# Windowed attention and a gated feed-forward: two weight loads moved in the queue, one normalising pass for two head pairs, diagonals on two engines, and a new table of order

## Chip, core and metric

One core of a Trainium2 chip. Five engines run side by side: TensorE (PE) multiplies matrices into PSUM, VectorE (DVE), ScalarE (ACT) and GpSimd (POOL) work elementwise, SyncE (SP) issues transfers. The metric is the device time of one execution in microseconds (us).

## What is computed

The kernel takes q, k and v (8 batches, 8 heads, 576 positions, 64 wide) and three weights, and gives 8 x 576 x 512 numbers.

```python
# attention: window of 32 positions to each side
scores = q @ k.T / 8
scores = where(abs(i - j) <= 32, scores, -1e9)
attn   = exp(scores - max) ; attn /= sum(attn) + 1e-9
x      = (attn @ v), heads side by side            # (8, 576, 512)
# feed-forward with a convolution of three positions in the gate
h    = relu(x @ w_in)                              # w_in: 512 x 1024
c    = conv_w[0]*h[s-1] + conv_w[1]*h[s] + conv_w[2]*h[s+1]
out  = (h * sigmoid(c)) @ w_out                    # w_out: 1024 x 512
```

## The kernel before

**Attention** (`attention`, L755) runs for one batch at a time, in two halves `s` of 288 positions. SP loads q and k (`load_qk`, L494, two loads for each half) and v (`load_v`, L524) in float32 into staging tiles `qst`, `kst` and `vst`. `cast_qk`, `cast_v` and `shift_v` turn them into bf16 tiles `qn`, `kn`, `ve` and `vo`, where `vo` is v moved by 64 rows; for batch 0 any of three engines may do it, later POOL alone. `transposes` (L583) turns q and k on PE (L597) and copies them from PSUM into `qT` and `kT`. `scores` (L624) multiplies a tile of 64 queries by 128 keys on PE (L657). The mask is put on in one of three ways: PE adds a band before the exp (L646), or POOL or DVE multiplies by a 0/1 mask after it (L679). ACT takes the exp (L672) into `attn`. `values` (L682) multiplies by v with a column of ones beside it (L700), so that the sum of a row stands in column 64 of 65. DVE takes the reciprocal (L719) and multiplies each of the two head pairs of a PSUM slot by it, one pass for each (L722), into `xn`. `turn` (L729) transposes `xn` into `xT`: on PE (L744) for batches 0 and 1, by a transfer (L735) for the others.

**Feed-forward** (`hidden`, L797) runs over 12 chunks of 384 positions, three chunks for two batches. Chunks 0 and 1 are cut into two pieces. For each of eight blocks `m` of 128 channels, PE multiplies `xT` by `w_in` (L835), ACT takes the relu into `hT` (L851), and the three taps of the convolution are dealt out in one of six ways (`KINDS`, L792): PE with a diagonal matrix (L872), ACT with a scale (L902), DVE by multiply and add in PSUM (L909), or POOL in `tmp` (L888, L893). ACT takes the tanh (L914; the sigmoid as a tanh of half the argument) and DVE forms the gate (L917) into `gT`. `project` (L929) multiplies by `w_out` on PE (L940), copies the result to `y` (L395 or L401), and SP writes it out (L960, L956).

The diagonals (24 matrices of 128 x 128, `diag_w`) are built at the start by `conv_weights` (L468, L483) on DVE. `load_w` (L558) loads w_in and w_out in two halves each into the staging tiles `wst` and casts them (L578). `copy` (L393) does all copies and casts, so in the profile L395 is ACT, L397 POOL and L401 DVE.

**What sets the order.** All of this only records operations with what they read and write. Four tables at the top then fix everything: `ORDER` (the order in which operations are issued, L29), `PICK` (the engine of those that have a choice), `BANKS` (the PSUM bank of each slot) and `CHOICE` (the way of the mask or of the taps). `Plan.place` (L263) walks through `ORDER`, gives each operation an engine and a bank and computes a start time by costs written beside each operation; the instructions are then issued in order of these start times, so the costs decide how the queues interleave. Each engine works through its queue in that order and waits on semaphores for what it needs. `warm` (L966) puts spare matmuls (L969) where PE would stand idle in the first 36 us of the plan. SP's loads go through one queue, with eight semaphores in turn: a transfer waits for the one eight places before it. A load into a staging tile also waits until the tile's last contents have been cast.

In the first part of SP's queue stand q and k of both halves of batch 0, v of both halves (six loads), then the two halves of w_in as the 15th and 16th load. The loads of batch 1 and of w_out follow.

Of the kernel before, what the change touches and what calls it, by code (L numbers as in the profile page):

```python
# [9 lines left out]
FP32 = mybir.dt.float32  # L10
BF16 = mybir.dt.bfloat16
AF = mybir.ActivationFunctionType
ALU = mybir.AluOpType
# [4 lines left out]
    0, 0, 0, 0, 0, 2, 0, 2, 0, 2, 5, 5, 0, 0, 5, 5, 5, 5, 5, 5, 5, 5, 5, 0, 5, 5, 2, 2, 2, 0, 0, 5,  # L18
    5, 5, 1, 5, 5, 5, 5, 2, 5, 5, 5, 1, 0, 5, 2, 0, 0, 0, 0, 0, 2, 2, 3, 2, 0, 2, 1, 3, 0, 1, 2, 2,
    1, 5, 0, 3, 0, 0, 0, 2, 2, 2, 2, 3, 2, 2, 0, 2, 3, 0, 2, 2, 0, 1, 2, 2, 1, 4, 2, 0, 2, 3, 0, 5,  # L20
    3, 2, 2, 0, 2, 0, 0, 2, 0, 2, 2, 3, 2, 3, 2, 2, 1, 2, 3, 2, 2, 0, 2, 1, 2, 2, 2, 0, 2, 3, 3, 1,
    2, 3, 3, 2, 2, 2, 3, 2, 2, 3, 2, 0, 2, 2, 3, 2, 3, 2, 2, 3, 0, 2, 2, 3,
]
SUPERSET = False
WARM = (5.0, 36.0)
# [4 lines left out]
    27, 34, 28, 35, 45, 46, 0, 1, 2, 3, 10, 30, 29, 36, 37, 51, 17, 26, 25, 14, 24, 22, 49, 52, 50,  # L30
    47, 48, 5, 12, 23, 11, 70, 69, 72, 77, 76, 87, 88, 7, 55, 56, 32, 42, 79, 71, 78, 89, 90, 93,
    91, 92, 53, 54, 94, 99, 100, 95, 96, 4, 97, 98, 39, 31, 38, 13, 33, 44, 16, 41, 21, 43, 61, 73,
    80, 62, 64, 57, 58, 59, 9, 60, 63, 65, 67, 74, 81, 75, 82, 84, 15, 83, 40, 85, 86, 105, 115,
    117, 116, 119, 101, 102, 66, 68, 118, 224, 225, 220, 221, 106, 108, 20, 107, 226, 227, 242, 222,
    223, 103, 120, 122, 124, 230, 231, 121, 228, 229, 234, 235, 246, 104, 111, 123, 232, 233, 250,
    236, 18, 243, 247, 244, 112, 6, 19, 248, 8, 113, 114, 237, 238, 138, 135, 142, 145, 137, 144,
    153, 136, 143, 155, 156, 151, 239, 249, 259, 253, 152, 251, 256, 154, 245, 240, 252, 241, 109,
    157, 158, 260, 261, 176, 177, 140, 182, 183, 194, 195, 257, 258, 110, 266, 267, 190, 191, 392,
    393, 162, 163, 396, 397, 386, 387, 262, 263, 159, 160, 388, 389, 390, 264, 265, 394, 398, 274,
    400, 270, 402, 391, 275, 401, 254, 271, 395, 405, 399, 408, 411, 161, 412, 268, 416, 139, 149,  # L40
    146, 147, 419, 406, 255, 409, 422, 403, 413, 404, 420, 410, 281, 278, 417, 418, 421, 414, 423,
    425, 179, 178, 310, 311, 284, 415, 424, 317, 141, 282, 283, 407, 269, 150, 164, 165, 287, 290,
    285, 286, 167, 166, 426, 427, 168, 169, 170, 171, 328, 279, 280, 291, 324, 325, 313, 312, 318,
    326, 327, 174, 175, 172, 272, 273, 288, 276, 277, 184, 185, 192, 196, 173, 428, 429, 297, 289,
    329, 430, 330, 300, 444, 431, 148, 293, 298, 292, 301, 130, 134, 132, 449, 331, 197, 445, 299,
    302, 294, 450, 446, 447, 451, 448, 193, 295, 296, 180, 188, 131, 186, 133, 125, 128, 126, 127,
    129, 303, 304, 351, 314, 319, 350, 355, 362, 363, 366, 432, 433, 335, 332, 333, 349, 348, 354,
    364, 367, 360, 361, 365, 334, 475, 336, 337, 203, 204, 368, 201, 202, 369, 307, 308, 476, 181,
    187, 189, 315, 320, 322, 316, 323, 338, 339, 342, 198, 199, 205, 340, 341, 436, 437, 200, 440,
    441, 434, 435, 452, 343, 453, 454, 442, 458, 443, 321, 455, 345, 344, 438, 439, 483, 482, 485,  # L50
    489, 496, 463, 497, 459, 500, 467, 460, 461, 484, 490, 498, 502, 503, 352, 358, 464, 462, 468,
    501, 469, 456, 457, 465, 466, 521, 520, 525, 305, 306, 536, 537, 532, 353, 357, 359, 518, 519,
    524, 534, 530, 531, 499, 506, 507, 533, 535, 206, 207, 209, 208, 371, 372, 210, 211, 373, 374,
    504, 505, 538, 539, 370, 212, 356, 375, 213, 376, 378, 379, 542, 543, 377, 487, 492, 380, 382,
    486, 494, 491, 381, 540, 541, 488, 495, 508, 509, 510, 512, 218, 219, 214, 215, 216, 217, 470,
    511, 513, 515, 514, 523, 527, 493, 522, 528, 529, 526, 544, 545, 546, 547, 548, 549, 559, 560,
    555, 556, 571, 557, 471, 550, 551, 472, 558, 473, 563, 561, 562, 564, 588, 572, 576, 474, 569,
    570, 573, 574, 682, 683, 689, 719, 718, 724, 734, 735, 477, 478, 684, 685, 690, 702, 703, 700,
    567, 589, 577, 590, 591, 723, 721, 720, 581, 582, 725, 583, 584, 585, 575, 568, 593, 736, 737,
    565, 566, 608, 701, 602, 592, 607, 609, 610, 687, 692, 383, 594, 586, 603, 595, 597, 479, 604,  # L60
    605, 732, 733, 347, 384, 346, 623, 596, 598, 587, 621, 696, 624, 641, 480, 622, 599, 578, 697,
    642, 698, 699, 629, 630, 600, 625, 626, 730, 731, 637, 606, 601, 633, 656, 627, 611, 638, 643,
    612, 613, 862, 823, 686, 694, 631, 688, 824, 830, 841, 693, 579, 580, 634, 664, 837, 628, 644,
    632, 842, 657, 691, 635, 636, 665, 614, 616, 658, 666, 645, 646, 667, 695, 825, 826, 831, 838,
    651, 647, 648, 652, 653, 309, 615, 649, 650, 669, 668, 659, 639, 640, 660, 654, 655, 743, 744,
    617, 618, 619, 839, 840, 745, 740, 706, 727, 670, 671, 741, 742, 661, 843, 844, 707, 738, 739,
    704, 705, 722, 726, 728, 729, 750, 751, 385, 753, 752, 517, 1025, 516, 757, 1027, 827, 863, 672,
    746, 747, 748, 749, 662, 758, 867, 845, 846, 878, 879, 663, 708, 709, 710, 847, 848, 712, 713,
    714, 763, 761, 764, 711, 673, 762, 790, 759, 760, 849, 715, 765, 766, 828, 835, 1026, 553, 832,
    1032, 1043, 833, 1044, 829, 834, 861, 836, 850, 1028, 860, 795, 674, 851, 853, 854, 855, 852,  # L70
    778, 675, 773, 755, 481, 676, 1033, 857, 856, 779, 796, 774, 767, 768, 866, 876, 877, 1045,
    1046, 677, 771, 769, 780, 781, 775, 776, 678, 784, 783, 785, 786, 787, 772, 800, 788, 770, 797,
    798, 791, 864, 870, 756, 1170, 1029, 554, 810, 809, 811, 1041, 804, 777, 782, 801, 1042, 792,
    799, 802, 793, 679, 680, 812, 813, 805, 789, 806, 807, 803, 874, 875, 552, 899, 900, 1064, 1065,
    1069, 808, 903, 904, 814, 907, 905, 1039, 901, 915, 906, 925, 908, 794, 865, 871, 930, 931, 932,
    815, 916, 1080, 1081, 902, 1076, 1077, 920, 816, 868, 620, 1030, 926, 917, 918, 1040, 927, 928,
    933, 934, 919, 929, 921, 935, 936, 922, 817, 818, 819, 1049, 1050, 1047, 1048, 1051, 872, 913,
    914, 717, 1031, 1035, 1037, 1038, 923, 909, 910, 873, 1034, 1056, 1052, 911, 912, 869, 1036,
    820, 937, 946, 821, 1053, 716, 754, 1057, 1059, 1055, 1054, 1058, 924, 947, 951, 952, 1062, 859,
    1210, 885, 886, 883, 884, 1063, 1068, 953, 954, 887, 955, 942, 938, 939, 940, 943, 944, 965,  # L80
    966, 1078, 1079, 941, 967, 968, 969, 970, 1074, 1075, 880, 881, 945, 948, 892, 893, 894, 895,
    971, 972, 1066, 1172, 1171, 1173, 1178, 988, 981, 949, 982, 882, 950, 983, 989, 985, 984, 1087,
    1088, 956, 975, 976, 973, 1186, 1177, 1188, 990, 991, 974, 1174, 1067, 1071, 992, 1072, 888,
    1190, 1000, 957, 986, 1187, 1191, 1189, 958, 977, 1175, 681, 959, 1070, 1073, 889, 891, 890,
    1089, 993, 1001, 987, 1002, 1084, 1085, 1082, 1083, 1180, 994, 1086, 1003, 1004, 960, 1094,
    1095, 1096, 1090, 1005, 961, 979, 995, 822, 1211, 978, 1208, 1209, 1176, 898, 858, 1212, 1179,
    1214, 1182, 1215, 980, 1183, 1181, 1184, 1185, 1009, 1097, 996, 997, 998, 1091, 1093, 1092,
    1099, 896, 1098, 1100, 897, 962, 963, 1060, 1006, 999, 1010, 1101, 1102, 1118, 1107, 1117, 1119,
    1120, 1224, 1195, 1007, 1108, 1225, 1121, 1011, 1196, 1105, 1106, 1130, 1014, 1008, 1015, 1197,
    1016, 1017, 1103, 1104, 1226, 1222, 1223, 1012, 1220, 1221, 1113, 1111, 1112, 1114, 1136, 1109,  # L90
    1110, 1129, 1131, 1132, 1133, 1013, 1227, 1122, 1202, 1203, 1205, 1115, 1116, 1151, 1020, 1018,
    1157, 1218, 1156, 1158, 1159, 1213, 1217, 1137, 1138, 1139, 1204, 1123, 1152, 1124, 1125, 1021,
    1141, 1022, 1019, 1153, 1154, 1126, 1127, 1134, 1142, 1146, 1023, 1024, 1061, 1219, 1155, 1128,
    1143, 1147, 1192, 1193, 1144, 1135, 1247, 1248, 1160, 1249, 1250, 1230, 1253, 1255, 1231, 1148,
# [951 lines left out]
```

## Time and profile before

| what | us |
|---|---|
| median of 13 runs | 224.06 |
| lowest and highest run | 222.55, 226.05 |
| the profiled run | 224.06 |
| its span in the profile | 222.2 |
| PE busy (share of the span) | 201.3 (91%) |
| DVE busy | 192.8 (87%) |
| ACT busy | 185.9 (84%) |
| POOL busy | 182.7 (82%) |
| loads and stores moved | 45.92 MB, 207 GB/s on the mean |

The profile is that of one execution. Busy time of PE counts a matmul from its start to its modelled end, so neighbours overlap and a busy PE need not be at its peak. In a row of instructions the busy time is the union of the row's instructions, and the mean in ns is that of one instruction alone; where instructions follow each other directly, busy time divided by their number is a little less than the mean. The clock of PE was granted at full speed except in the stretch from 10 to 20 us (0.83).

### The profile page before, as it was taken

The numbers are of one execution on the slowest core, as the hardware profiler recorded it, in microseconds if no ns is written. First come the engines' busy times: TensorE is split into PE (matmuls) and PEld (weight loads), VectorE is DVE, ScalarE is ACT, GpSimd is POOL, SyncE is SP. The second block draws the span as 40 slices with busy tenths as digits, with TensorE's granted clock in tenths as the row PEclk, the third lists the DMA queues.
The fourth block names the chain that finished last, engine by engine and source line by source line (L and its number), as shares of the span: only waits on it lengthen the run. The fifth ranks groups of instructions, "written<-read, shape, count | busy, mean of one in ns | idle before, by whom it ended". The sixth has DMA issues, their size and how long they took to land.

```text
span 222.2 us, 6471 instructions
## 1 busy us (share of the span) xinstructions
PE 201.3 (91%) x2451; PEld 127.0 (57%) x2469; DVE 192.8 (87%) x430; ACT 185.9 (84%) x388; POOL 182.7 (82%) x234
## 2 busy tenths in 40 slices
PE   1768899888999799999999999789999999999994
PEld 0535688775677566646655556446646555455542
DVE  6769794797698799999999989799999999999970
ACT  2239679777989599999899989988999989999962
POOL 4267577979889989799999998999998999999930
PEclk9997999999999999999999999999999999999999
DMA  5999999998998899999999989963537313130334
GB/s 175 302 181 388 361 274 331 307 236 247 290 185 244 261 150 230 338 216 204 246 228 249 230 205 273 342 194 78 83 83 256 101 62 118 25 143 3 142 117 167
DMA packets 68675, 45.92 MB, mean 207 GB/s; under 512 B 53644, under 2 KB 53924, under 8 KB 68644
## 3 DMA queue, kind: packets, MB, share of 16 engines
q1 hardware_dynamic: 68608, 45.49, 78.9%
q8 instruction: 19, 0.31, 0.6%
q14 instruction: 12, 0.10, 0.1%
q10 hardware_dynamic: 36, 0.01, 0.0%
HBM read 32.52 MB, written 9.44 MB: 189 GB/s over the span
## 4 chain that ended last, share of the span: by engine, by line
PE 37%; POOL 14%; DVE 12%; DMA 11%; SPq 6%; ACT 3%; issue 3%; POOLq 0%; DVEq 0%; ACTq 0%
PE ps_all L835 16%; PE ps_all L940 14%; DMA kst<-in_k_dram 7%; POOL vo L397 4%; POOL ve L397 3%; POOL kn L397 3%; DVE gT L917 3%; DVE ps_all L909 3%; DMA vst<-in_v_dram 3%; PE ps_all L872 2%; DMA qst<-in_q_dram 2%; SPq L497 2%; SPq L735 2%; POOL qn L397 2%; PE ps_all L700 2%
## 5 line engine op out<-in xcount | busy, mean ns | idle before, releaser
L835 PE MATMUL ps_all<-xT,w_in_sb 128*128 128x385 bf16 (+4 forms) x448 | 72.6, 305 | 1.6 <-DVE xn L722 0.5
L909 DVE SCALAR_TENSOR_TENSOR ps_all<-hT,conv_w_sb,ps_all 128x384 f32<-128x384 bf16 (+2 forms) x115 | 64.5, 594 | 3.0 <-PE ps_all L872 1.8
L940 PE MATMUL ps_all<-w_out_sb,gT 128*128 128x512 bf16 (+1 forms) x278 | 65.0, 373 | 1.1 <-issue 0.2
L851 ACT ACTIVATE hT<-ps_all 128x385 bf16<-128x385 f32 (+4 forms) x112 | 47.4, 453 | 7.6 <-PE ps_all L835 7.1
L835 PEld LDWEIGHTS <-w_in_sb 128*128 128x128 bf16 x448 | 40.6, 98 | 22.6 <-issue 1.3
L917 DVE SCALAR_TENSOR_TENSOR gT<-ps_all,hT 128x384 bf16<-128x384 f32 (+3 forms) x112 | 51.6, 491 | 1.4 <-ACT ps_all L914 0.8
L940 PEld LDWEIGHTS <-gT 128*128 128x128 bf16 x296 | 28.3, 98 | 29.5 <-issue 0.5
L893 POOL TENSOR_TENSOR tmp<-tmp 128x384 f32<-128x384 f32 x41 | 41.2, 1007 | 2.3
L672 ACT ACTIVATE attn<-ps_all 128x1024 bf16<-128x1024 f32 (+1 forms) x40 | 36.5, 941 | 6.9 <-PE ps_all L657 6.4
L888 POOL TENSOR_SCALAR tmp<-hT,conv_w_sb 128x384 f32<-128x384 bf16 x62 | 37.1, 607 | 2.5 <-ACT hT L851 0.6
L914 ACT ACTIVATE ps_all<-ps_all 128x384 f32<-128x384 f32 (+3 forms) x92 | 36.9, 432 | 1.7 <-PE ps_all L872 0.8
L397 POOL TENSOR_SCALAR vo<-vst 64x1024 bf16<-64x1024 f32 (+1 forms) x33 | 32.8, 994 | 5.7 <-DMA vst<-in_v_dram 3.3
L722 DVE TENSOR_TENSOR xn<-ps_all,rec 128x256 bf16<-128x256 f32 (+1 forms) x64 | 28.5, 483 | 0.8
L397 POOL TENSOR_SCALAR ve<-vst 128x512 bf16<-128x512 f32 (+1 forms) x38 | 24.6, 657 | 1.4 <-DMA vst<-in_v_dram 0.4
L397 POOL TENSOR_SCALAR qn<-qst 128x1152 bf16<-128x1152 f32 (+1 forms) x18 | 18.5, 1032 | 7.8 <-DMA qst<-in_q_dram 6.1
L395 ACT COPY y<-ps_all 128x512 f32<-128x512 f32 (+1 forms) x36 | 21.0, 591 | 4.1 <-PE ps_all L940 3.8
L397 POOL TENSOR_SCALAR kn<-kst 128x1152 bf16<-128x1152 f32 (+1 forms) x18 | 19.1, 1066 | 6.2 <-DMA kst<-in_k_dram 4.2
L902 ACT ACTIVATE ps_all<-hT,conv_w_sb 128x384 f32<-128x384 bf16 (+1 forms) x42 | 23.8, 584 | 0.2
L395 ACT COPY kT<-ps_all 128x512 bf16<-128x512 bf16 (+1 forms) x19 | 14.3, 751 | 9.5 <-PE ps_all L597 9.0
L872 PE MATMUL ps_all<-hT,diag_w 128*128 128x192 bf16 (+3 forms) x117 | 18.5, 270 | 0.9 <-DVE gT L917 0.5
L679 DVE TENSOR_TENSOR attn<-attn,mask 128x1024 bf16<-128x1024 bf16 (+1 forms) x16 | 15.9, 996 | 3.6 <-ACT attn L672 3.4
L597 PE MATMUL ps_all<-ident,qn 128*128 128x128 bf16 x144 | 13.5, 227 | 5.8 <-DVE qn L401 4.5
(64 smaller groups left out, 228.3 us busy)
## 6 DMA issues: line engine op xcount, KB each, us to landing
qst<-in_q_dram SPq DMA_DIRECT2D x32, 288.0 KB, 5.2
kst<-in_k_dram SPq DMA_DIRECT2D x32, 288.0 KB, 5.4
out_dram<-y SPq DMA_DIRECT2D x11, 768.0 KB, 5.3
vst<-in_v_dram SPq DMA_DIRECT2D x23, 256.0 KB, 5.8
vst<-in_v_dram SPq DMA_DIRECT2D x16, 192.0 KB, 6.3
wst<-in_moe_w_in_dram SPq DMA_DIRECT2D x2, 1024.0 KB, 6.8
wst<-in_moe_w_out_dram SPq DMA_DIRECT2D x2, 1024.0 KB, 10.9
out_dram<-y SPq DMA_DIRECT2D x2, 256.0 KB, 2.0
```

The costliest lines, as they stand in the source:

```text
L395: nc.scalar.copy(out=out_, in_=in_)
L397: nc.gpsimd.tensor_scalar(out=out_, in0=in_, scalar1=1.0, scalar2=0.0, op0=ALU.mult, op1=ALU.add)
L672: add(act(2 * w), t + 0.1, lambda e: nc.scalar.activation(at, ps(sl, 0, 1024).rearrange("p (e x) -> p e x", e=2)[:, :, 0:w], AF.Exp, bias= ...
L722: add(dve(2 * n * D), t + 0.1, lambda e, y=y: nc.vector.tensor_tensor(out=xn[i][:, cs[0]:cs[0] + n].rearrange("p c (e g) d -> p c e g d", ...
L835: nc.tensor.matmul(ps(sl, 0, n), w_in_sb[:, kc, m * 128:(m + 1) * 128], x_[:, kc, a0:a1], start=(kc == 0), stop=(kc == KC - 1),)
L851: nc.scalar.activation(o_, i_, AF.Relu, bias=0.0, scale=0.5)
L888: add("POOL", tt + 0.05, lambda e, m=m, tv=tv, n_=n_, ks=by_pool: nc.gpsimd.tensor_scalar(out=tv(n_ > 0), in0=hview(m, o0, o1, ks[n_] - 1) ...
L893: add("POOL", tt + 0.05, lambda e, tv=tv: nc.gpsimd.tensor_tensor(out=tv(), in0=tv(), in1=tv(1), op=ALU.add,), reads=[("tmp", r, True)], w ...
L909: add("DVE", tt + 0.1, lambda e, m=m, n_=n_, pv=pv, ks=by_dve: nc.vector.scalar_tensor_tensor(out=pv(), in0=hview(m, o0, o1, ks[n_] - 1), ...
L914: add(act(no), tt + 0.2, lambda e, pv=pv, tv=tv, alone=alone: nc.scalar.activation(pv(), tv() if alone else pv(), AF.Tanh, bias=0.0, scale=1.0
L917: add(dve(no), tt + 0.3, lambda e, m=m, mid=mid, i2=i2, pv=pv: nc.vector.scalar_tensor_tensor(out=gT[ig][:, m, o0:o1].rearrange("p (i x) - ...
L940: nc.tensor.matmul(ps(sl, f0, f1), gT[ig][:, m, 128 * i:128 * i + 128], w_out_sb[:, m, f0:f1], start=(m == 0), stop=(m == MB - 1),)
```

## The change

1. **Order of the first loads.** v of half 1 of batch 0 (three loads) goes behind w_in. The first load is a q load of half 1, and the second part of q of half 0 becomes the fifth. w_in is the 12th and 13th load, w_out comes two loads earlier than before.
2. **One normalising pass.** In `values` the two head pairs of a PSUM slot are multiplied by their reciprocals in one instruction of 4·n·64 elements over two banks, where there were two of 2·n·64 (n is 2 for half 0 and 3 for half 1).
3. **Diagonals.** Each of the 24 may be built by DVE or by ACT; the table gives 18 to ACT and 6 to DVE.
4. **POOL's taps.** `tmp` becomes one tile of six buffers: five for results, one shared for the second product (three times two before). The products and sums of two taps are recorded as one operation. The way in which PE, POOL and DVE shared a block (the fifth of six) is gone.
5. **Copies of the result.** Every copy of a projection to `y` may go to ACT or DVE; five whole ones and the last half go to DVE, where only the last half did.
6. **Code for pairs of blocks** (`PAIR`, two blocks in one relu, tanh or gate) is there with thresholds of 99, so that no chunk or batch uses it.
7. **Costs and tables.** The costs that stand beside the operations are changed (below), and `ORDER`, `PICK`, `BANKS`, `CHOICE` and `TIMES` are new as a whole. The two programs have in all 432 and 380 DVE instructions, 391 and 416 on ACT, 236 and 230 on POOL, 2470 and 2461 matmuls, 156 and 156 entries in SP's queue, each counted with the program's own branch and the like.

```diff
@@ TIMES, conv_weights
     "load": [
         "qk00",
         "qk11",
+        "v00",
+        "qk01",
+        "w_in1",
+        "w_in0",
+        "w_out1",
+        "v01",
+        "qk10",
         "v11",
         "v10",
-        "w_in1",
-        "qk01",
-        "v00",
-        "v01",
-        "w_out1",
         "w_out0",
-        "w_in0",
-        "qk10",
     ],
...
-                    nc.vector.tensor_scalar(
-                        out=o_, in0=ident, scalar1=w_, scalar2=None, op0=ALU.mult
-                    )
-                add(("DVE", 0.17), 10.0 + m, diag, ...)
+                    if e == "ACT":
+                        nc.scalar.activation(o_, ident, AF.Copy, bias=0.0, scale=w_)
+                    else:
+                        nc.vector.tensor_scalar(
+                            out=o_, in0=ident, scalar1=w_, scalar2=None, op0=ALU.mult
+                        )
+                add({"DVE": 0.33, "ACT": 0.29}, 10.0 + m, diag, ...)
@@ costs
-        return ("DVE", n / 1920.0 + 0.2)
-    def pool(n):
-        return ("POOL", 0.00089 * n + 0.14)
+        return ("DVE", n / 1920.0 + 0.35)
+    def pool(n, tap=False):
+        return ("POOL", 0.00089 * n + (0.215 if tap else 0.14))
...
-        base = 0.0146 * 2 * len(todo)
+        base = 0.0165 * 2 * len(todo)
...
-        for on, y, cost in (("POOL", 1, 0.00188 * 2 * w + 0.155), ("DVE", 2, 2 * w / 1920.0 + 0.25)):
+        for on, y, cost in (("POOL", 1, 0.00188 * 2 * w + 0.155), ("DVE", 2, 2 * w / 1920.0 + 0.5)):
@@ values
-        add(("DVE", 0.105), t + 0.1, lambda e: nc.vector.reciprocal(rv, view()[:, :, :, D]),
+        add(("DVE", 0.126), t + 0.1, lambda e: nc.vector.reciprocal(rv, view()[:, :, :, D]),
             reads=[sl], writes=[("rec", r)], slots=[sl], group=gr)
-        for y in range(2):
-            add(dve(2 * n * D), t + 0.1, lambda e, y=y: nc.vector.tensor_tensor(
-                out=xn[i][:, cs[0]:cs[0] + n].rearrange("p c (e g) d -> p c e g d", e=2)[:, :, :, g0 + y],
-                in0=view(y)[:, :, :, 0:D],
-                in1=rv[:, y].rearrange("p (c e) -> p c e", e=2).unsqueeze(3).broadcast_to([128, n, 2, D]),
-                op=ALU.mult,
-            ), ...)
+        add(dve(4 * n * D), t + 0.1, lambda e: nc.vector.tensor_tensor(
+            out=xn[i].rearrange("p c (e g) d -> p (c e) g d", e=2)[:, 2 * cs[0]:2 * (cs[0] + n), g0:g0 + 2],
+            in0=view()[:, :, :, 0:D].rearrange("p y r d -> p r y d"),
+            in1=rv.rearrange("p y r -> p r y").unsqueeze(3).broadcast_to([128, 2 * n, 2, D]),
+            op=ALU.mult,
+        ), ...)
@@ hidden (taps on POOL), project
-    tmp = [pp.tile([128, 2, CH], FP32, name=f"tmp{i}") for i in range(3)]
+    NTB = 5
+    tmp = pp.tile([128, NTB + 1, CH], FP32, name="tmp")
...
+                    def taps(e, m=m, tv=tv, ks=ks, begin=ks == by_pool[:2]):
+                        for z, kk in enumerate(ks):
+                            own = begin and z == 0
+                            nc.gpsimd.tensor_scalar(
+                                out=tv(not own), in0=hview(m, o0, o1, kk - 1), scalar1=conv_w_sb[:, kk, m:m + 1],
+                                scalar2=0.0, op0=ALU.mult, op1=ALU.add,
+                            )
+                            if not own:
+                                nc.gpsimd.tensor_tensor(out=tv(0), in0=tv(0), in1=tv(1), op=ALU.add)
...
-            on = act(f1 - f0)
-            if end and f0:
-                on = dve(f1 - f0)
+            on = dict([act(f1 - f0), dve(f1 - f0)])
```

## The prediction

> **What bounds the kernel now.** I read three views in this order: the busy time of each engine by stretch, the chain that ended last, and the order of time in the first 60 us. The stretches (columns: stretch, its length, then PE, PE loads, DVE, ACT, POOL busy with instruction counts, clock, DMA share, GB/s):
>
> ```profile
> 0.00:60.00 60.00, 47.58 (x708) 35.21 (x712) 45.22 (x130) 39.55 (x89) 41.97 (x63) 0.97 1.01 280
> 60.00:143.00 83.00, 78.99 (x1107) 50.84 (x1111) 76.96 (x165) 77.09 (x154) 75.00 (x88) 1.00 1.04 239
> 143.00:222.20 79.20, 74.73 (x638) 40.94 (x647) 70.64 (x136) 69.29 (x147) 65.75 (x85) 1.00 0.38 116
> ```
>
> From 60 us on no engine alone is the bound: PE, DVE, ACT and POOL are idle 8.5, 14.6, 15.8 and 21.4 us of 162, part of it in the last seven. In the first 60 us they are idle 12.4, 14.8, 20.5 and 18.0. So a fifth to a third of the opening is empty and little of the rest. The chain says what ends last (start, length, what):
>
> ```profile
> 74.69 5.15 DMA kst<-in_k_dram
> ...
> 200.59 3.45 PE ps_all L940 x16
> 204.05 3.94 PE ps_all L835 x24
> 207.99 0.33 PE ps_all L872 x2
> 208.37 9.49 PE ps_all L940 x47
> 217.89 1.05 PE ps_all L940 x8
> 219.01 0.42 DVE y L401
> ```
>
> It is PE almost without a gap from 143 us; loads and POOL's casts from 69 to 143 us; DVE, PE and ACT before that. PE's work at the end cannot shrink by much, so time is to be had where work could start earlier. What holds the opening, in order of time:
>
> ```profile
> 13.70 1.63 SPq L568 DMA_DIRECT2D wst<-in_moe_w_in_dram  x2
> 20.65 1.78 POOL L397 TENSOR_SCALAR w_in_sb<-wst 128x512 bf16<-128x512 f32 x3 [1.32 <-DMA wst<-in_moe_w_in_dram]
> 23.12 1.07 ACT L395 CAST xT<-ps_all 128x512 bf16<-128x512 f32 x2
> 24.24 1.03 PE L835 MATMUL ps_all<-xT,w_in_sb 128*128 128x256 bf16 x8
> ```
>
> The first feed-forward matmul starts at 24.24: its weights come at 20.65, its activations at 24.19.
>
> **Part 1: w_in behind half 0 of batch 0.** SP issues w_in as its 15th and 16th load now and as its 12th and 13th after: the three loads of v for half 1 (128+256+192 = 576 KB) go behind it. Over 0 to 20 us the DMA moves 245 GB/s, in 20 to 40 us 334, so w_in lands 576/334 = 1.7 to 576/245 = 2.35 us earlier; I take 2.0, hence 18.6 and, with the second half 3.07 us behind as now (23.72 against 20.65), 21.7. But q of half 0 is moved too: its second part becomes the fifth load (a q of half 1 goes first). The sixth load now is cast at 9.87, as it lands, so the fifth is there by then. From 10.0: ACT cast 0.7, PE and copies of qT to 12.0, scores 0.5, the first exp to 14.3; then two diagonals and two v casts in ACT's queue (1.9), the second exp 1.0, values 0.3: 17.5. On DVE two reciprocals and two merged passes (1.7) and two xT copies (1.3): first matmul at about 20.7, **3.5 us earlier**. The ends: 19.7 if the two v casts and diagonals between the exps cost half, 24.2 (no gain) if ACT's five early casts, each behind a landing, hold the first exp back by 3.5 us, the 2.97 us that it waited for scores now and a little more.
>
> What is late next: v of half 1. It now follows 2 MB of w_in and a q; 8 q/k loads, 576 KB, 2 MB, 288 KB and 576 KB are 5.8 MB, at 245 GB/s 24 us, 25 with the start. Until then PE, ACT and DVE have piece 0 (32 matmuls 4.1 us, eight relu and eight tanh of 0.39 and 0.34: 5.8 us of ACT). Half 1: values at 27, two merged passes 2.2, transposes and copies 1.5: its matmuls at 31, now 34.25, 3.2 earlier. One v cast on DVE stands between the first gates and waits for that landing: up to 1.5 us of DVE, hidden by the 9 us that DVE is lighter by (part 3). I carry **-3.3**. Past these loads all transfers have the same bytes, and no later step of SP's queue gets longer.
>
> **Part 2: one normalising pass per two head pairs.** Rows of DVE:
>
> ```profile
> L722 DVE TENSOR_TENSOR xn<-ps_all,rec 128x384 bf16<-128x384 f32 x32 | 16.4, 551 | 0.4
> L722 DVE TENSOR_TENSOR xn<-ps_all,rec 128x256 bf16<-128x256 f32 x32 | 12.2, 415 | 0.4
> L483 DVE TENSOR_SCALAR diag_w<-ident,conv_w_sb 128x128 bf16<-128x128 bf16 x24 | 6.8, 324 | 0.1
> L902 ACT ACTIVATE ps_all<-hT,conv_w_sb 128x384 f32<-128x384 bf16 x40 | 23.0, 591 | 0.2
> L902 ACT ACTIVATE ps_all<-hT,conv_w_sb 128x192 f32<-128x192 bf16 x2 | 0.9, 442 | 0.0
> L679 POOL TENSOR_TENSOR attn<-attn,mask 128x512 bf16<-128x512 bf16 x2 | 2.3, 1154 | 0.7 <-ACT attn L672 0.7
> ```
>
> Busy per pass is 0.512 and 0.381 us, 1.02 ns an element, 0.12 fixed. Doubled: 0.905 and 0.643. 32 passes of 24.8 us replace 64 of 28.6: **-3.8 us of DVE**, plus about 1 us of issue gaps. The strided walk over two banks has no row; it could eat the whole 3.8, and cannot save more than the fixed 3.8.
>
> **Part 3: diagonals partly by ScalarE, and the rest of the re-dealt work.** 18 of 24 diagonals go to ACT. DVE loses 18 x 0.283 = 5.1. On ACT the nearest rows are the taps, which also scale by a vector: 442 at 192 elements, 591 at 384, so 392 at 128, or 0.33 busy when they follow each other: +5.9. The Trainium skill speaks against this: "ScalarE: Activation LUTs", Rules for kernel authors, sends plain multiplies to VectorE, up to about 3 times faster per element in bf16. By that rule a diagonal on DVE would be a third of ACT's, an estimate of 0.13, and each move would lose 0.26 us, 18 of them 4.7, with DVE lighter by only 2.3. The row of this trace has 324 ns on DVE; by the rows the move loses 18 x 0.07 = 1.2 us and frees 5.1 of DVE, and ACT is idle 12.8 us of its first 20, where most of these go. I take the rows.
>
> The table also re-deals work (counts of the two programs, each times its row). DVE: other casts -0.7, four transposed copies fewer net -3.3, conv taps -1.0, five y copies of about 0.66 more +3.3. ACT: five q/k casts +3.4, four more transposed copies +3.1, taps +2.4, y -3.0, xT -1.1, one v cast +0.6. POOL: eight scalings (-4.8) and five sums (-5.0) of 384 fewer, five of 255 more (+2.8), two w_in and qn casts -2.0, five masks +9.6 (four of 1024 at 2.1 each, a little under twice the 512 row). PE: eight band matmuls of 512 (0.16 each) and two of 256 fewer, conv matmuls +0.4: -1.1. With the overlap of neighbours taken out:
>
> DVE 192.8 to 184; **ACT 185.9 to 195.7**; POOL 182.7 to 183; PE -1.1. The four together change by +0.5 us: work is moved and not saved.
>
> Where it falls, by summing both queues up to the same gates: up to the last relu of chunk 2 ACT carries 67.2 for 58.7 and DVE, up to that chunk's gates, 66.2 for 77.2. After it ACT has 128.4 for 127.1 and DVE 118.1 for 115.8. So the opening is lighter on DVE by 11 and heavier on ACT by 8.5, and the rest is as long as before, -1.1 (PE) to +2.3 (DVE). ACT's +8.5 is hidden by its idle time: it finished those relus at 86.0 us with 27.3 us idle, and breaks even with 18.8. If that cover is gone, each further us of ACT idle costs one. For the rest I take 0.
>
> **Sum.** Span 222.2 - 3.3 = 218.9, and the profiled run's 224.06 lies 1.86 above its span: **220.8 us**. The profiled run is at the median of the 13 runs (224.06).
>
> **Rivals.**
> *ACT becomes the bound (slower).* Place: ACT's queue up to chunk 2. Five casts and 18 diagonals stand in order before and between the exps, each cast waiting for a landing; an exp behind a late one holds values, normalising and the first matmuls. Price: 8.5 us less the idle time they fill. If idle time falls only from 27.3 to 22.3, chunk 2 is late by 3.5: 225.7 span, 227.5 us. It decides above 18.8 us of idle time. For it: ACT carries 195.7 of a 222 us span, most of all engines. Against: 15.7 of its idle is in the first 30 us, exactly where the new work stands. **226 us**, somewhere inside.
>
> *The staging loop hides it (same).* From 69 to 143 us the chain runs through loads, SP and POOL's casts; DMA share is 1.04 and POOL has 75.0 of 83. Neither gets lighter. If this loop paces everything, an earlier opening is waited away: **224 us**. Against: the last scores stand at 152 of PE's 188 us of net work (columns at the chain's rates, four L835 of 385 in 0.66 us), some 40 us behind the last loads, so loads lead.
>
> *The new table also closes stalls (faster still).* Its costs are raised for DVE against POOL (mask on DVE +0.25 us, diagonal 0.17 to 0.33), and the rows (1047 ns, 324 ns) are near the new ones. If it takes 4 of DVE's 14.6 and ACT's 15.8 us of idle after 60 us: **217 us**. Against: nothing in the trace of before shows it.
>
> **How the numbers follow.** Forecast 0.50, ACT bound 0.22, hidden 0.15, stalls closed 0.13. The forecast's own range is 218.5 to 223; with the rivals 216.5 to 226.5. A measurement of this kernel can tell about 0.3% from no change. Faster: nearly all of the forecast, the fourth case and a part of the third, 0.63; within 0.3%: 0.11; slower: the ACT case and slips of the others, 0.26.
>
> **What would show it.** Right: first w_in matmul at 20 to 22 us; merged passes near 0.93 and 0.68 us; ACT busy 194 to 197, DVE 183 to 186; chunk 2's relus done near 82.5; the stretch from there to the end unchanged at about 136 us. Wrong: ACT at over 95% from 20 us on with PE waiting for exps or relus; a first matmul past 23 us; a merged pass above 1.05 us; DVE waiting for v of half 1 by more than 2 us; the end of the last loads unmoved with PE idle before it.

## The result, and the profile after

| | before | after |
|---|---|---|
| median, us | 224.09 (48 runs) | 221.59 (11 runs) |
| lowest and highest | 222.52, 226.42 | 220.68, 223.28 |
| profiled run, its span | 224.06, 222.2 | 221.66, 219.9 |

The ratio is **0.9897, 95% interval 0.9868 to 0.9926**: 1% faster. It compares the fast executions alone (44 of the 48 before, all 11 after), hence 2.3 us where the medians differ by 2.5. The forecast was 220.8, with a range of 218.5 to 223.

The page of the changed kernel, part 1 (busy time of each engine, its share of the span, instructions):

```profile
span 219.9 us, 6446 instructions
PE 200.9 (91%) x2442; PEld 124.5 (57%) x2460; DVE 185.1 (84%) x378; ACT 193.4 (88%) x413; POOL 184.0 (84%) x228
```

Its busy time by the same three stretches (columns as in the prediction):

```profile
0.00:60.00 60.00, 49.62 (x738) 37.11 (x743) 41.31 (x111) 49.87 (x124) 40.19 (x63) 1.00 1.01 279
60.00:143.00 83.00, 80.45 (x1066) 48.49 (x1074) 78.74 (x144) 77.78 (x152) 78.23 (x86) 1.00 1.01 230
143.00:219.90 76.90, 70.87 (x641) 38.87 (x644) 65.00 (x125) 65.79 (x141) 65.56 (x81) 1.00 0.45 131
```

In the first 60 us PE does 2.0 us more than before, ACT 10.3 more, DVE 3.9 and POOL 1.8 less. The opening in order of time (start, length, what, and in brackets the idle time before it and what ended it):

```profile
11.42 1.14 SPq L575 DMA_DIRECT2D wst<-in_moe_w_in_dram  x2
...
19.56 1.20 POOL L401 TENSOR_SCALAR w_in_sb<-wst 128x512 bf16<-128x512 f32 x2 [2.58 <-DMA wst<-in_moe_w_in_dram]
...
19.98 1.29 DVE L405 CAST xT<-ps_all 128x512 bf16<-128x512 f32 x2 [0.79 <-PE ps_all L752]
...
21.42 1.47 PE L855 MATMUL ps_all<-xT,w_in_sb 128*128 128x256 bf16 x12 [0.43 <-DVE xT L405]
```

The first feed-forward matmul is 2.8 us earlier (24.24 before). The 40th relu in ACT's order is the last of chunk 2, so it is a mark that both kernels pass. Before, and after:

```profile
85.53 0.52 ACT L851 ACTIVATE hT<-ps_all 128x385 bf16<-128x385 f32 x1
```
```profile
82.15 0.51 ACT L875 ACTIVATE hT<-ps_all 128x385 bf16<-128x385 f32 x1
```

It ends at 82.66 us, where it ended at 86.05. So 3.4 us are won by then, and of these only 2.3 reach the end: from the mark to the end it takes 137.2 us, where it took 136.2. What is left to do behind the mark, before and after (columns as in the prediction):

```profile
86.05:222.20 136.15, 129.84 (x1313) 74.42 (x1324) 124.32 (x245) 124.37 (x256) 117.61 (x146) 1.00 0.67 173
```
```profile
82.66:219.90 137.24, 129.93 (x1307) 73.02 (x1316) 121.82 (x233) 124.58 (x258) 122.12 (x144) 1.00 0.72 181
```

PE and ACT have about the same work left (0.1 and 0.2 us more), DVE 2.5 us less and POOL 4.5 more.

The chain that ended last has changed its face. By engine, from the pages of before and after:

```profile
PE 37%; POOL 14%; DVE 12%; DMA 11%; SPq 6%; ACT 3%; issue 3%; POOLq 0%; DVEq 0%; ACTq 0%
```
```profile
POOL 51%; PE 19%; issue 7%; ACT 6%; DMA 5%; SPq 5%; DVE 5%; POOLq 1%; ACTq 0%; DVEq 0%
```

And its last pieces before the projection (start, length, what):

```profile
208.52 1.14 POOL tmp L918 x2
...
209.73 1.01 POOL tmp L923
...
212.52 0.50 ACT ps_all L953
...
213.66 1.49 PE ps_all L995 x10
```

PE led this chain before; now it is POOL with its taps, up to the last tanh, gate and projection.

### The profile page after: what moved, and what is told of

The parts are those of the page before. It is cut to its first block, busy times and chain, and to the rows that moved or that the text cites. A ratio compares the mean times of both kernels' runs of the same rounds, so it can differ in the third digit from the quotient of the medians.

```text
span 219.9 us, 6446 instructions
## 1 busy us (share of the span) xinstructions
PE 200.9 (91%) x2442; PEld 124.5 (57%) x2460; DVE 185.1 (84%) x378; ACT 193.4 (88%) x413; POOL 184.0 (84%) x228
## 4 chain that ended last, share of the span: by engine, by line
POOL 51%; PE 19%; issue 7%; ACT 6%; DMA 5%; SPq 5%; DVE 5%; POOLq 1%; ACTq 0%; DVEq 0%
POOL tmp L923 13%; POOL tmp L918 12%; POOL vo L401 8%; PE ps_all L995 7%; POOL ve L401 6%; PE ps_all L855 5%; DMA wst<-in_moe_w_in_dram 5%; POOL attn L689 4%; SPq L504 4%; POOL qn L401 4%; POOL kn L401 4%; PE ps_all L607 2%; ACT ps_all L953 2%; ACT hT L875 2%; PE ps_all L930 1%
## 5 line engine op out<-in xcount | busy, mean ns | idle before, releaser
L943 DVE SCALAR_TENSOR_TENSOR ps_all<-hT,conv_w_sb,ps_all 128x384 f32<-128x384 bf16 (+3 forms) x114 | 64.4, 595 | 3.8 <-PE ps_all L930 2.5
L953 ACT ACTIVATE ps_all<-ps_all 128x384 f32<-128x384 f32 (+3 forms) x93 | 39.8, 447 | 0.6 <-PE ps_all L930 0.3
L923 POOL TENSOR_TENSOR tmp<-tmp 128x384 f32<-128x384 f32 (+1 forms) x38 | 37.7, 991 | 3.2
L918 POOL TENSOR_SCALAR tmp<-hT,conv_w_sb 128x384 f32<-128x384 bf16 (+1 forms) x57 | 33.5, 595 | 1.8 <-ACT hT L875 0.3
L938 ACT ACTIVATE ps_all<-hT,conv_w_sb 128x384 f32<-128x384 bf16 (+1 forms) x46 | 26.8, 597 | 0.2
L730 DVE TENSOR_TENSOR xn<-ps_all,rec 128x512 bf16<-128x512 f32 (+1 forms) x32 | 25.8, 818 | 0.6
L399 ACT COPY y<-ps_all 128x512 f32<-128x512 f32 (+1 forms) x31 | 18.0, 599 | 5.0 <-PE ps_all L995 4.9
L399 ACT COPY kT<-ps_all 128x640 bf16<-128x640 bf16 (+1 forms) x23 | 17.3, 762 | 1.8 <-PE ps_all L667 1.0
L710 PEld LDWEIGHTS <-attn 128*64 128x64 bf16 x640 | 12.6, 111 | 8.4 <-issue 2.9
L710 PE MATMUL ps_all<-ve,attn 128*64 128x65 bf16 x384 | 15.1, 197 | 1.6 <-DVE attn L689 0.8
```

The source lines that it names most:

```text
L399: nc.scalar.copy(out=out_, in_=in_)
L710: nc.tensor.matmul(ps(sl, lo, lo + D + 1, 64 * j, 64 * j + 64), attn[a][:, 512 * h_ + col:512 * h_ + col + 64], (vo if tt % 2 else ve)[i][ ...
L918: nc.gpsimd.tensor_scalar(out=tv(not own), in0=hview(m, o0, o1, kk - 1), scalar1=conv_w_sb[:, kk, m:m + 1], scalar2=0.0, op0=ALU.mult, op1 ...
L923: nc.gpsimd.tensor_tensor(out=tv(0), in0=tv(0), in1=tv(1), op=ALU.add)
L943: add("DVE", tt + 0.1, lambda e, m=m, y=y, n_=n_, pv=pv, ks=by_dve: nc.vector.scalar_tensor_tensor(out=pv(y), in0=hview(m, o0, o1, ks[n_] ...
L953: nc.scalar.activation(o_, i_, AF.Tanh, bias=0.0, scale=1.0)
```

## What was to be told apart

My theory after the result: the gain is the earlier opening, and POOL, which the chain names for half of the span, now sets the end. Rival 1: the new table does it and the named parts are worth nothing. Rival 2: the lighter DVE (merged pass, diagonals) carries the gain. Four runs undo or shift one thing on the new table, two pairs and one all three; three put parts on the old table; two leave masks out (some keys outside the window then stay in). Every ratio is to the kernel before on the same chip; "against after" divides it by 0.9897, and 0.001 is 0.22 us. The two intervals together leave such a difference uncertain by about 1 us (1.4 us for the two kernels that leave masks out).

## Experiments

**One part undone, tables kept.**

`a_two_pass` gives each head pair a pass of its own again:

```diff
-        add(dve(4 * n * D), t + 0.1, lambda e: nc.vector.tensor_tensor(
...
+        def norm(e):
+            for y in range(2):
+                nc.vector.tensor_tensor(
+                    out=xn[i][:, cs[0]:cs[0] + n].rearrange("p c (e g) d -> p c e g d", e=2)[:, :, :, g0 + y],
+                    in0=view()[:, y].rearrange("p (c e) x -> p c e x", e=2)[:, :, :, 0:D],
+                    in1=rv[:, y].rearrange("p (c e) -> p c e", e=2).unsqueeze(3).broadcast_to([128, n, 2, D]),
+                    op=ALU.mult,
+                )
+        add(dve(4 * n * D), t + 0.1, norm,
...
```

> The changed kernel with its tables, but each head pair normalised by a pass of its own again (64 passes where there are 32); DVE becomes 2.7 us heavier (28.6 us of such passes before, 25.9 after), some 0.6 us of it in the first 60 us. Theory (the earlier start of the opening carries the gain, POOL sets the end): DVE is not what ends last, so +0.2 to +1.0 us on the changed kernel's 221.6. Rival 1 (the new table does it, the named parts are worth nothing): within 0.4 us of the changed kernel. Rival 2 (the merged pass carries the gain): +2 us or more, back to about 224.

Measured: 0.9870 (0.9829 to 0.9911), against after -0.6 us with overlapping intervals. DVE was busy 186.9 instead of 185.1 us. This lies below all three ranges that were written, but by less than the uncertainty. The merged pass alone is worth nothing that can be measured. Rival 2 falls for this part.

`a_diag_dve` takes the entries of the 24 diagonals out of the table of engines:

```diff
-            e = op.eng = PICK.get(op.idx) or next(iter(op.on))
+            e = op.eng = (op.idx not in range(3, 27) and PICK.get(op.idx)) or next(iter(op.on))
```

> The changed kernel with its tables, but all 24 diagonals on DVE again: ACT 18 x 0.36 = 6.5 us lighter and DVE 18 x 0.28 = 5.1 us heavier, all before 35 us. Theory: DVE idles 4 to 5 us in the first 20 us of the changed kernel, the rest delays the normalising and the copies of xT, so the first feed-forward matmul comes 0 to 1.5 us later and the end 0.3 to 1.5 us later. Rival 1: within 0.4 us. Rival 2 (this part carries the gain): +2 us or more. The rule that sends plain multiplies to VectorE would have it faster than the changed kernel, by up to 1 us.

Measured: 0.9905 (0.9870 to 0.9941), against after +0.2 us. Alone it is worth nothing that can be measured either; the gain of up to 1 us that the page's rule would give does not show.

`a_v_first` puts the order of these loads back (`mv` are the three loads of v for half 1 of batch 0, `WL` those of the weights, w_in first):

```diff
...
-    steps = [(op.start, op.idx, op.run, op.eng) for op in order]
+    at = {op.idx: op.start for op in order}
...
+    for z, i in enumerate(mv):
+        at[i] = min(at[x] for x in WL[:2]) - 0.01 * (len(mv) - z)
+    steps = [(at[op.idx], op.idx, op.run, op.eng) for op in order]
```

> The changed kernel with its tables, but the three loads of v for half 1 of batch 0 are issued just before w_in, as in the kernel before. 576 KB at 245 to 334 GB/s ahead of w_in: it lands 1.7 to 2.4 us later. Theory: the first feed-forward matmul moves from 21.4 to 23.0 to 23.8 us and the end by +1.0 to +2.2 us. Rival 1: within 0.4 us, since half 1 gains what half 0 loses. If the loads are not what held the first matmul (the 8-back semaphore or the scores did), it moves by less than 0.5 us.

Measured: 0.9947 (0.9914 to 0.9981), against after +1.1 us, as the theory had it for the end, though hardly more than the uncertainty. The way there was another: w_in was first cast at 20.89 instead of 19.56, 1.3 us later and not 1.7 to 2.4, and the first matmul came only 0.4 us later, at 21.85. That is the range written for "the loads are not what held the first matmul": in the changed kernel it waits for its activations (21.27), and only here for its weights (21.80). The rest fell on the later blocks (first gate 28.02 for 26.87).

**Does POOL set the end?** `a_masks_dve` sends the seven masks of POOL to DVE:

```diff
+        if CHOICE[pick] == 1:
+            CHOICE[pick] = 2
         added = CHOICE[pick] == 0
```

> The changed kernel with its tables, but the seven masks that POOL multiplies (four of 1024 columns at 2.1 us, three of 512 at 1.27 us: 12.3 us of POOL between 51 and 155 us) go to DVE at the same places of the order, about 4 x 0.95 + 3 x 0.45 = 5.2 us. Theory (POOL is on the chain from 63 to 212 us and ends last): 1.5 to 4 us faster than the changed kernel, 217.5 to 220, until PE or DVE takes over. Rival (what the chain shows is one of several equal queues, DVE and PE bind as much): within 0.5 us or slower by up to 2 us.

Measured: 1.0031 (0.9999 to 1.0064), 3.0 us slower than after, which is worse than even the rival's "up to 2 us". The theory falls in its second half. POOL had 12 us less to do (172.1), yet its taps still ended the chain. The list of waits of this kernel (who waited for what: us in total, times, longest) has one that had been 0.3 us in the changed kernel:

```profile
POOL tmp L920 <- ACT hT L877: 8.8, 4, 3.4
```

POOL now stood idle for ACT's relus, with 26.42 of 37 us busy from 143 to 180 us, where after has 35.29. What made the relus late was not followed further. To separate the relief of POOL from the load on DVE, two kernels leave masks out:

```diff
-            add(on, t + 0.2, lambda e: ENG[e].tensor_tensor(out=x_, in0=x_, in1=m_, op=ALU.mult),
+            add(on, t + 0.2, lambda e: e != "POOL" and ENG[e].tensor_tensor(out=x_, in0=x_, in1=m_, op=ALU.mult),
```

(and the same with "DVE").

> The changed kernel without the seven masks that POOL multiplies (left out, so that some keys outside the window are not masked): POOL 12.3 us lighter between 51 and 155 us, nothing else changed. If POOL sets the end, as the chain has it: 1.5 to 4 us faster than the changed kernel. If POOL only follows the relus of ACT: within 0.7 us. It tells which half of the run with the masks on DVE was felt, the relief of POOL or the load on DVE.

Measured: 0.9811 (0.9757 to 0.9864), 1.9 us faster than after, for 12.3 us of POOL. That is inside the range written for "POOL sets the end". But part of it is not the masks: in its profiled execution the 65th matmul by w_in started at 35.54, 0.9 us ahead of the changed kernel's (36.48) and long before the first of these masks at 51 us. Behind the 40th relu it was 1.1 us faster.

> The changed kernel without the sixteen masks that DVE multiplies (left out, so that some keys outside the window are not masked): DVE 15.2 us lighter between 15 and 181 us. If DVE is the engine that the others wait for at those places (seven masks of 5.2 us put on it cost 3.0 to 3.7): 4 us or more faster than the changed kernel. If the four queues are even, so that taking from one alone gains little while adding to one costs: 0.5 to 2 us faster.

Measured: 0.9731 (0.9677 to 0.9786), 3.7 us faster than after, for 15.2 us of DVE. It misses both ranges and lies nearer the first (4 us or more), within its uncertainty of it. Taking work from one engine gave 0.15 us (POOL) and 0.25 us (DVE) for each us. Putting 5.2 us of masks on DVE cost 4.9 against the kernel without POOL's masks (1.0031 against 0.9811), nearly one for one. So no single queue is the bound: relief of either is worth about a quarter of itself or less, though DVE's more than POOL's, and the chain named POOL. That the queues are evenly loaded is the reading that fits; it was not tested in another way.

**All three parts undone, table kept**, to see what the table alone does: the three diffs above together. What stays is all else of the change: the order, the engines and banks, POOL's taps, the copies of the result, the other moves of loads.

> The changed kernel's tables with all three named parts undone at once: two normalising passes per slot, all diagonals on DVE, v of half 1 ahead of w_in. Theory (what the opening loses is carried to the end one for one, and the losses of the single undoings, 0 to 0.1, 0.2 to 0.7 and 1.1 to 1.3 us, add up, a little more where they meet on DVE): +1.3 to +2.3 us on the changed kernel, 223.0 to 224.0; the table then accounts for the rest, 0.2 to 1.2 us. Rival 1 (the new table does it): +1.0 us at most, 222.6 or less. Rival 2 (the three parts are all of it): +2.5 us or more, 224.1 and above.

Measured: 1.0017 (0.9986 to 1.0049), against after +2.7 us. Rival 1 falls: the new table without the three parts is as slow as the kernel before. The loss lies in the range written for the three parts being all of the gain. My theory missed too, since the single undoings add up to 0.7 us and not to 2.7, though that sum is uncertain by about 2.

Where it is lost can be read on DVE. The changed kernel, DVE in order of time from the second half of w_in to the first gate:

```profile
23.03 1.99 DVE L405 CAST w_in_sb<-wst 128x512 bf16<-128x512 f32 x3 [1.10 <-DMA wst<-in_moe_w_in_dram]
24.93 1.30 DVE L490 TENSOR_SCALAR diag_w<-ident,conv_w_sb 128x128 bf16<-128x128 bf16 x3
...
26.87 0.41 DVE L970 SCALAR_TENSOR_TENSOR gT<-ps_all,hT 128x255 bf16<-128x255 f32 x1
```

The same place with all three parts undone:

```profile
24.95 1.99 DVE L406 CAST w_in_sb<-wst 128x512 bf16<-128x512 f32 x3 [2.10 <-DMA wst<-in_moe_w_in_dram]
26.86 2.58 DVE L491 TENSOR_SCALAR diag_w<-ident,conv_w_sb 128x128 bf16<-128x128 bf16 x6
...
30.07 0.41 DVE L977 SCALAR_TENSOR_TENSOR gT<-ps_all,hT 128x255 bf16<-128x255 f32 x1
```

The cast stands at the head of the queue and starts 1.9 us later, and six diagonals (2.58) stand between it and the first gate instead of three (1.30): 1.9 + 1.3 = 3.2 us. After it come, in the same queue, the passes of half 1. DVE is then full. Busy time from 25 to 35 us in the changed kernel (columns as above: PE, PE loads, DVE, ACT, POOL):

```profile
25.00:30.00 5.00, 4.43 (x80) 3.23 (x77) 4.90 (x13) 4.93 (x14) 4.67 (x8) 1.00 0.91 301
30.00:35.00 5.00, 4.65 (x93) 3.80 (x86) 3.84 (x8) 5.00 (x11) 4.74 (x9) 1.00 1.21 258
```

and with all three undone:

```profile
25.00:30.00 5.00, 2.94 (x35) 1.78 (x36) 5.00 (x11) 2.50 (x5) 4.67 (x7) 1.00 0.89 276
30.00:35.00 5.00, 4.52 (x85) 3.64 (x84) 4.87 (x14) 3.55 (x9) 4.65 (x9) 1.00 0.93 194
```

DVE is busy for 9.87 of 10 us and ACT for 6.05; in the changed kernel ACT has 9.93 and DVE 8.74, and PE 1.6 us more. A full DVE alone does not make the loss, however: `a_diag_dve`, which lost 0.2 us, has 9.87 there too (ACT 7.61, PE 0.7 us less than the changed kernel).

**Which parts meet?** Two pairs undone on the new table.

> The changed kernel with two parts undone: all diagonals on DVE and v of half 1 ahead of w_in; the merged pass stays. All three undone cost 2.7 us, the single ones 0, 0.2 and 1.1. In the trace with all three undone DVE waits 2.10 us for the second half of w_in at 24.95 us, and behind it stand six diagonals (2.58 us) ahead of the first gate. Theory (late weights and the diagonals behind them meet in DVE's queue between 22 and 35 us; the passes matter little): +2.0 to +2.8 us on the changed kernel, ratio to the kernel before 0.999 to 1.002. If the parts merely add: +1.3, ratio 0.995 to 0.996.

Measured: 1.0013 (0.9981 to 1.0045), against after +2.6 us.

> The changed kernel with the two parts on DVE undone, the load order kept: DVE is 6 to 7.8 us heavier and ACT 6 lighter. Theory (without the late weights DVE works off most of the diagonals between 10 and 20 us, where it is idle 4.3 us): +0.2 to +1.2 us on the changed kernel, ratio 0.990 to 0.995. If the load on DVE alone is what counts: +1.8 us or more, ratio 0.998 or above.

Measured: 0.9953 (0.9919 to 0.9988), against after +1.3 us, at the edge of what was expected, and by the times more than the two single undoings together.

Diagonals and load order undone together cost as much as all three. With these two undone the merged pass is worth nothing more (1.0017 against 1.0013). Whether the two cost more together than apart stays open. The times suggest it, 2.6 us against 0.2 and 1.1. But the single costs make a ratio of 0.9955 with an uncertainty of its own of about 0.006, and the pair's 1.0013 lies within what the two uncertainties allow. The traces speak for plain adding: the first gate comes 0.9 us later than in the changed kernel with the diagonals undone (27.81), 1.2 later with v first (28.02) and 1.9 later with both (28.77), and the end of the 40th relu 1.2, 1.3 and 2.7 later.

**The parts on the old table.** `b_all` has all three; `b_dve` the merged pass and the 18 diagonals on ACT (issued where DVE's stood in the order); `b_w_first` only the loads:

```diff
...
+    for z, i in enumerate(WL[:2]):
+        at[i] = min(at[x] for x in mv) - 0.01 * (2 - z)
```

> The kernel before with its own tables and the three named parts alone: one pass for two head pairs, the same 18 diagonals on ACT, w_in issued ahead of the three loads of v for half 1 of batch 0. DVE is 7.8 us lighter, ACT 5.9 heavier. In its order the work of half 1 stands ahead of the first pieces of the feed-forward, so the later v of half 1 (by 2 MB) holds values, normalising and the copies of half 1 with the feed-forward behind them. Theory (the order decides whether earlier weights are used): -1.0 to +1.5 us against the kernel before. Rival 2 (the parts carry the gain whatever the order): -2 us or more. If a lighter DVE is worth about half of what is taken off it, as the masks moved to it suggest (5.2 us for 3.0 to 3.7), up to -3.9.

> The kernel before with its own tables and load order, and the two parts that take work off DVE: one pass for two head pairs, 18 diagonals on ACT. DVE was busy for 9.97 us of the ten from 25 to 35 us there and ACT idle 15.7 us of its first 30. Theory (relief where DVE is full counts): 0.5 to 2.5 us faster than the kernel before, ratio 0.989 to 0.998. If the diagonals in ACT's queue hold the exps: slower by 0.5 to 2 us.

> The kernel before with its own tables, and only w_in issued ahead of the three loads of v for half 1 of batch 0. In its order the values of half 1 stand ahead of the feed-forward on PE and DVE; with all three parts the cast of that v came at 25 us, and the first feed-forward matmul at 28.3 instead of 24.2. Theory (the load order pays only with an order of work that takes the feed-forward first): slower by 3 to 5 us, ratio 1.013 to 1.022, as with all three parts or more. If what slowed the kernel with all three parts was the diagonals on ACT: within 0.7 us of the kernel before.

Measured: `b_all` 1.0148 (1.0096 to 1.0200), 3.3 us slower than before; `b_dve` 1.0011 (0.9970 to 1.0051), no change; `b_w_first` 1.0093 (1.0053 to 1.0133), 2.1 us slower. The loss of `b_all` is more than twice what my theory allowed (up to +1.5). Relief of a full DVE gave nothing, against my expectation. The load order alone costs time: the direction was as expected, the size below it. Why the first matmul is late can be read on POOL (order of time, `b_w_first`):

```profile
20.91 0.62 POOL L398 TENSOR_SCALAR ve<-vst 64x512 bf16<-64x512 f32 x1 [6.11 <-DMA vst<-in_v_dram]
...
24.48 2.36 POOL L398 TENSOR_SCALAR w_in_sb<-wst 128x512 bf16<-128x512 f32 x4
```

In the old order the casts of half 1's v stand ahead of those of w_in. POOL waits 6.11 us for a v that was moved back, and casts w_in at 24.48, where the kernel before did so at 20.65. Weights that land earlier (17.19 for 20.50) are used later. How this makes 2.1 us at the end is not shown: the profiled execution is the fastest of twelve (224.41 us, only 0.4 above that of before), its 40th relu ends 0.6 us later than before, and the other eleven took 225.66 us and more.

**One measure over all runs.** From the traces: the start of the first matmul by w_in, the end of the 40th relu, and the time from there to the end of the span (one profiled execution each, which may lie 2 us off its kernel's median).

| kernel | 1st w_in matmul | 40th relu ends | from there to the end | span |
|---|---|---|---|---|
| before | 24.24 | 86.05 | 136.2 | 222.2 |
| b_dve | 24.83 | 87.37 | 136.1 | 223.4 |
| b_w_first | 26.32 | 86.60 | 136.0 | 222.6 |
| b_all | 28.34 | 90.06 | 136.3 | 226.4 |
| after | 21.42 | 82.66 | 137.2 | 219.9 |
| a_two_pass | 21.05 | 83.69 | 138.0 | 221.7 |
| a_diag_dve | 22.04 | 83.87 | 137.2 | 221.1 |
| a_v_first | 21.85 | 84.00 | 136.7 | 220.7 |
| a_two_diag | 21.98 | 84.60 | 136.9 | 221.5 |
| a_diag_v | 22.10 | 85.37 | 136.8 | 222.1 |
| a_none | 22.34 | 86.92 | 137.0 | 223.9 |
| a_masks_dve | 21.54 | 84.41 | 140.0 | 224.4 |
| a_no_pool_masks | 20.98 | 81.72 | 136.1 | 217.8 |
| a_no_dve_masks | 21.95 | 82.05 | 135.2 | 217.3 |

Where the masks are left alone, the stretch behind the 40th relu has nearly the same length whatever happened ahead of it: 136.0 to 136.3 us with the old table, 136.7 to 138.0 with the new one. A us lost or won up to the mark reaches the end as nearly a us. And the new table's later part is about 0.9 us longer than the old one's. POOL's 4.5 us of extra work there fit this: the kernel without POOL's masks, with 111.85 us of POOL behind the mark instead of 122.12, is back at 136.1. They are not shown to be the cause. A table with the new opening and the old later part was not tried.

Another reason for the gain would be PE's clock: in the profiled execution of the kernel before it was at half speed for 3.4 us between 15 and 20 us, in that of the changed kernel it was not. But of the 80 executions of the kernel before that ran beside these experiments, 37 had a mean clock of 0.997 or more and took 224.2 us on the mean, 34 had 0.989 to 0.992 and took 224.4, and nine had less and took 226.2. All 80 together lie 0.3 us above the 37, so a clock that is always whole would account for about 0.3 us and not for 2.3.

## Why the prediction was right

**Sum.** "222.2 - 3.3 = 218.9": the 3.3 were there, 3.39 at the 40th relu, which the prediction had near 82.5 and which ended at 82.66. What failed is "For the rest I take 0": the rest took 1.0 us more. The prediction summed ACT, DVE and PE behind chunk 2 and not POOL, and POOL is where most was added (122.1 us of work for 117.6); whether that is the reason stays open. Hence 219.9 for 218.9, and 221.7 for 220.8.

**Part 1.** The mechanism was right and two terms were mis-sized. "w_in lands 2.0 us earlier": 1.1 for the first half (first cast at 19.56 for 20.65) and 0.7 for the second (23.03 for 23.72). SP issued w_in 2.3 us earlier (11.42 for 13.70), but from issue to landing it took 9.5 us on the median and 6.8 before. The place in the queue does not fix the landing: when the first half of w_in had landed at 19.48, 5.0 MB had been moved (256 GB/s), and the loads up to it are only 4.0. So about 1 MB of other bytes went ahead of its end, for the most part loads issued behind it. `b_w_first` has the same eleven loads ahead of w_in, and there it landed at 17.19 with 4.6 MB moved. So the same 576 KB were worth 3.3 us of landing on the old table (20.50 to 17.19) and 1.4 on the new one (20.87 in `a_v_first` to 19.48), around the prediction's 1.7 to 2.35. "First matmul at about 20.7": 21.42. Its activations came at 21.27, after its first weights (20.76).

"Half 1: its matmuls at 31, now 34.25" failed: the 33rd w_in matmul started at 33.48, 0.8 us earlier than before and not 3.2. The opening nevertheless reached its 3.3. The new order puts the feed-forward of half 0 first (first gate at 26.87 for 31.16); the 65th w_in matmul was 1.8 us earlier, and the 40th relu 3.4. That last growth is in no step of the prediction, so that its 3.3 was met so closely is in part luck. The place of w_in alone makes 1.3 us of it by the trace of `a_v_first`, and 1.1, give or take 1, at the end.

**Part 2.** The passes last 955 and 681 ns, where 0.93 and 0.68 us were named. By form (columns: busy us, mean ns, idle before):

```profile
L730 DVE TENSOR_TENSOR xn<-ps_all,rec 128x768 bf16<-128x768 f32 x16 | 15.3, 955 | 0.4
...
L730 DVE TENSOR_TENSOR xn<-ps_all,rec 128x512 bf16<-128x512 f32 x16 | 10.6, 681 | 0.2
...
L488 ACT ACTIVATE diag_w<-ident,conv_w_sb 128x128 bf16<-128x128 bf16 x18 | 6.5, 394 | 0.0
...
L490 DVE TENSOR_SCALAR diag_w<-ident,conv_w_sb 128x128 bf16<-128x128 bf16 x6 | 2.5, 438 | 0.0
```

Busy time fell from 28.6 to 25.9, by 2.7 and not 3.8: so about a us of the saving was lost, which the prediction had left to the strided walk over two banks. At the end it made no difference that could be measured.

**Part 3.** 394 ns for a diagonal on ACT, as taken from the taps' row (392). The 0.33 us of busy time that the prediction set beside it does not follow from the rows shown (0.45 busy for each at 192 elements and 0.575 at 384 make about 0.41 at 128); it was 0.36, 6.5 us in all for 5.9. The factor of up to about 3 for VectorE, which the prediction took from the page, was not reached here: 438 ns on the mean, and 242 at best. Totals: DVE 185.1 (184 forecast), ACT 193.4 (195.7, and just under its range of 194 to 197), POOL 184.0 (183). The prediction's own changes of the four engines add up to +0.2 us, not to +0.5, which changes nothing. The price that it put on the move was about right. The worth is small: in the trace the first gate comes 0.9 us later without the move, and in the times 0.2 us, give or take 1, are left of it.

**Rivals.** *ACT becomes the bound*: the place was right. ACT is full from 25 to 35 us. The price was nil: taking the diagonals off it again (`a_diag_dve`, ACT at 7.6 of these 10 us) gained nothing that could be measured. *The staging loop hides it*: no, the table above carries each us of the opening to the end, through the same loads. *The new table closes stalls*: no, its later part is longer. Not foreseen was that table and parts are worth something only together: about 0 for the table, +3.3 us for the parts, -2.3 for both.

## What to carry

An order of work and the order of its loads are one thing. Loads that were moved forward paid here only where the queues that cast and use them were ordered the same way; with the old order a load moved back stood at the head of a queue that still asked for it first. Where several queues are nearly full, the engine that the last chain names need not be the bound: test it by taking its work away before anything is moved off it. Here that gave about a quarter of a us or less for each us taken, while work put on an engine cost almost a whole us for each us added. A mark in the trace that all versions pass (here the 40th relu) splits a small change in the total into parts that are each large enough to read.

## What the runs showed of the hardware

**A diagonal on DVE lasts 0.24 us or 0.65.** In the changed kernel the two built while POOL runs nothing take 244 and 246 ns; three that start under a POOL operation take 603, 627 and 667, and each ends 52 or 53 ns after that operation does. One took 242 although POOL was at work for two thirds of it: it began 0.04 us before one POOL operation ended, and the next began 0.08 us after that end. The Trainium skill, "SBUF — State Buffer", SBUF: two separate sides, gives a reason that fits: VectorE in its two-port modes and GpSimd share one pair of ports, and the one that starts first holds it for its whole instruction. So the row's mean of 438 ns is a mix, and ACT's 394, which varied from 384 to 405 ns only, is a price that can be planned.

**The clock of PE falls in a wait of 2.5 us.** With all three parts on the old table PE has nothing from 22.6 to 25.07 us. Busy time and granted clock (the last but two column) there:

```profile
20.00:22.50 2.50, 1.63 (x27) 0.93 (x26) 1.83 (x4) 1.05 (x2) 0.00 (x0) 1.00 0.99 148
22.50:25.00 2.50, 0.10 (x2) 0.11 (x1) 0.00 (x0) 0.97 (x3) 1.83 (x3) 0.71 0.84 263
25.00:30.00 5.00, 3.89 (x57) 2.81 (x57) 2.01 (x4) 3.23 (x7) 4.76 (x9) 0.50 0.97 282
```

In windows of half a us the mean is 0.56 from 23.5 to 24.0 and 0.61 from 30.0 to 30.5: the clock halves at about 23.6 us, 1.0 us after the last matmul, and is whole again at 30.4. The Trainium skill, "TensorE: Matmul & The Clock Gate", What's actually happening, gives half rate after an idle window of about 3.4 us; the halving is as it says, the wait was shorter here. In the kernel before the clock was halved between 15 and 20 us (mean 0.66) with PE busy for 3.52 of the 5 us ahead and its longest wait there 1.04 us, so here it took no wait of 2.5 us. How much of the 3.3 us this makes was not separated. The mean clocks go the same way: 0.998 to 1.000 in all runs of the changed kernel, 0.982 to 0.992 in those of `b_all`, and in `b_w_first` 0.998 for the one run at 224.41 us and 0.977 to 0.992 for the eleven from 225.7 to 229.2.
